# Two blocks of dense experts' activations put between the last scores and the one-hot rows, and weight loads put ahead of the last gate stores

## The chip, the cores and the metric

The kernel runs on one core of a Trainium2 chip. The metric is device time in microseconds of one execution. The profile is that of one execution, taken by the hardware profiler; times in it count from the start of its span. The engines are PE (matrix multiplication), DVE (vector), ACT (activation), POOL and SP; here SP only issues DMAs.

## The reference

For 2,048 tokens of 512 values the kernel computes `x + A(layernorm(x)) + B(layernorm(x))`. A is attention with 32 heads of 16 that share one key and one value head. B is a layer of 4,096 single-neuron experts: each token has, for each of 32 heads, two rows of 64 scores; the top two of each row give four candidate experts, the best two of these are kept, and

```python
g = _softmax(top_s, axis=-1)
ue = u[top_e]
ve = v[top_e]
act = _gelu(jnp.einsum("nd,nhkd->nhk", xf, ue))
out = jnp.einsum("nhk,nhk,nhkd->nd", g, act, ve)
```

All inputs and outputs are float32. Matmuls run on operands split into a high and a low half, three products (`TERMS`) for one.

## The kernel before

**Tiling.** The tokens are 16 tiles of 128, in four groups of four. Attention is a sequence of double steps (`att_steps`): 4 score matmuls (L318, `sc`), exponentials on ACT (L321, `pt`), 16 matmuls of probabilities with values (L332, `pv`) as the trace counts them, 4 more scores. In each step `mid()` puts out DVE's and ACT's work for the experts, and `fill()` lets a generator, `score_thread` (run by `run_scores`), put out PE's: so many matmuls for a step as the costs it yields (`yield cost`) leave room for, `yield None` ending the step's share. Instructions are written in this order by hand (`tc.manual_schedule`); no scheduler moves them. `STORES` is a list of DMAs that SP is to issue at the start of a following step. SP issues in order; in the built program its DMAs take turns on eight semaphores, so that an issue waits for the DMA eight before it.

**Experts, two ways.** The score thread computes for each group the scores in eight chunks (`item`, `psc` L532), of which DVE takes the top two (L545, L547, `batch`); `gates` (L635 to L643) forms the softmax. Groups 0 and 1 then gather the rows of u and v for each token and expert (POOL, L883), DVE multiplies and sums (`dots` L895, `adds` L930). These go on beside everything else: the dots' pace is the variable `pos`. Groups 2 and 3 are dense instead (`dense`): every token meets all 4,096 experts, in 32 blocks of 128, each weighted by a gate that is mostly zero. So the trace has two dense groups; the texts call them the first and the second.

**A dense group.** (1) After the last scores the indices and gates are transposed (`ptd`, L714) and copied into `tr` (L715). POOL first copies an index table `io` (L704). (2) For 32 stretches of 16 tokens DVE makes one-hot rows (`oa` L725; `ob` L727, times the gate L728) and PE multiplies them (`pg`, L752, 16 matmuls each): a gate for each token and expert. ACT copies these (`gst`, L757), and SP stores them to DRAM, eight pairs of 512 KB in runs of 256 bytes (L760); behind the last pair it loads the gates of the first blocks (`gy`, L675) and x (`da`, L739). (3) For each block: raw weights `rw` (L657, L658; two buffers, so raw 2 is loaded when raw 0 is split) are split by ACT (L687, high) and DVE (L688, low) into `wk`; 12 matmuls contract x with u (`pact`, L799); ACT and DVE form gelu and gate (Square L821, L822, times the gate L825, tanh L842, L828, halves of `wd` L831 and L835); and after each pair of blocks the sums with v (`pout`, L783, L786). Blocks 0 and 1 are split in the steps of the last two one-hot products (`later_split`). Attention's output goes through `pwo` (L427), added on DVE (L433) to partial sums that SP loads (`fin`, L420).

**Lists.** `BEHIND` is DVE's work that follows the next dots; `ON_ACT`, `LAST`, `LATER` and `LATER_ACT` hold ACT's work for this or the next step; `POST` the copies out of a product. `dense_on` tells `mid` which stage runs. The buffers in question: `wk` (8; also `io`, `tr` and the one-hot rows), `wqt` (2, raw weights), `gy` (3), `wd` (4, also `gst`), and three banks `x` of PSUM for `psc`, `ptd`, `pg`, `pact`, `pout` and `pwo`.

Of the kernel before, what the change touches and what calls it, by code (L numbers as in the profile page):

```python
# [23 lines left out]
P = 128  # L24
# [30 lines left out]
def tile_kernel(ctx, tc, x, wq, wkv, wo, wqT, kT, uv, ub, vb, out):  # L55
# [17 lines left out]
    d_w = [dram.tile([P, KC, 2, 512], F32, name=f"dw{c}") for c in range(NC)]  # L73
    d_g = dram.tile([NB, P, 512], F32, name="dg")
# [481 lines left out]
    DT = []  # L556
# [7 lines left out]
    def batch(ph, c, b):  # L564
# [52 lines left out]
        if c == 0:  # L617
            DT.clear()
            dense_tiles()
# [14 lines left out]
        def gates():  # L634
            V.tensor_scalar(den, ex, 2.0, 2.0, op0=OP.mult, op1=OP.add)  # L635
            gg = T("gd", F32, [P, BT, 8])
            gv = gg.rearrange("p t (h k) -> p t h k", k=2)
            V.reciprocal(gv[:, :, :, 0], den)
            V.tensor_mul(gv[:, :, :, 1], ex, gv[:, :, :, 0])
            gh = T("gh", F16, [P, BT, 8])  # L640
            V.tensor_scalar(gh, gg, GS, None, op0=OP.mult)
            V.tensor_copy(dgt[:, :, 0, w], gh)
            stt(dgt[:, :, 1, w], gg, GS, gh, op0=OP.mult, op1=OP.subtract)  # L643

# [3 lines left out]
    def dense(DG, after):  # L648

        df1, df2, dgt = DT[:3]  # L650
# [12 lines left out]
        def gate_tile(b):  # L663
            if b not in gates:
                gy = late[0].tile([P, 2, 512], F32, name="gy", tag="gy", bufs=3)
                gates[b] = gy
            return gates[b]

        def fetch_gates(b):
            if b < NB and b not in fetched:  # L670
                if formed[0] < b - 2:

                    store(lambda: fetch_gates(b))
                    return
                nc.sync.dma_start(gate_tile(b)[:, 0, :], d_g[b])  # L675
                fetched.add(b)

        splits, halved = {}, set()

        def split(b):  # L680
            if b < NB:
                if b not in raws:
                    run(STORES)
                rw = raws.pop(b)
                us, vs = wk_tile(), wk_tile()
                for i, w in enumerate((us, vs)):
                    nc.scalar.copy(w[:, 0, :], rw[:, i, :])  # L687
                    behind(lambda w=w, i=i: nc.vector.tensor_tensor(out=w[:, 1, :], in0=rw[:, i, :], in1=w[:, 0, :],  # L688
                                                                    op=OP.subtract))
                behind(lambda: halved.add(b))  # L690
                splits[b] = us, vs
# [11 lines left out]
        io = kt(F16, (P, P, TB))  # L703
        nc.gpsimd.tensor_copy(io, iota_h[:, :, None].to_broadcast([P, P, TB]))  # L704
        fetch(0)
        fetch(1)
        yield None
        tr = kt(F16, (P, 3, 512))
        for n, src in enumerate((df1, df2, dgt)):
            if n == 2:  # L710
                yield None
            p = xtile("ptd")
            for j in range(GT):
                nc.tensor.transpose(p[:, j * P:(j + 1) * P], src[:, j].rearrange("p r s -> p (r s)"), ident)  # L714
            nc.scalar.copy(tr[:, n, :], p)  # L715
            yield 0.45
        dense_on[0] = 2
# [3 lines left out]
        def onehot(q):  # L721
            if q < NQ:
# [3 lines left out]
                ob = kt(F16, (P, NB, TB))  # L726
# [4 lines left out]
        def first_gates():  # L731

            fetch_gates(0)
            fetch_gates(1)
# [6 lines left out]

        onehot(0)
        onehot(1)
        for q in range(NQ):
# [10 lines left out]
            def copies(pv_=pv_, st=st, ql=ql, t0=t0):  # L755
                for hb in range(2):
                    nc.scalar.copy(st[hb][:, :, ql * TB:(ql + 1) * TB], pv_[:, 16 * hb:16 * hb + 16, :])  # L757
                if ql == 3:
                    for hb in range(2):
                        store(lambda hb=hb: nc.sync.dma_start(  # L760
                            d_g[16 * hb:16 * hb + 16, :, t0:t0 + 64].rearrange("b p t -> p b t"), st[hb]))
# [11 lines left out]
        def sums():  # L773
# [4 lines left out]
            for j in range(GT):  # L778
                p = xtile("pout")
                n = 0  # L780
                for wd, vs in ready:
                    for a, c in TERMS:
                        nc.tensor.matmul(p, wd[:, a, j * P:(j + 1) * P], vs[:, c, :], start=n == 0, stop=n == 5)  # L783
# [7 lines left out]
        for b in range(NB):  # L791
            if b not in halved:
                flush()
            us, vs = splits.pop(b)
            p = xtile("pact")
            n = 0
            for k in range(KC):
                for a, c in TERMS:
                    nc.tensor.matmul(p, us[:, a, k * P:(k + 1) * P], XT[DG][k][:, c, :],  # L799
                                     start=n == 0, stop=n == 11)  # L800
                    n += 1
# [4 lines left out]
                if k == KC - 1 and b == NB - 1 and after is not None:  # L806
                    wp_read(after, range(2))
                if b == NB - 1 and after is not None:
                    load_phase2_xt(SEQ[after][0], k)
                if k < KC - 1:  # L810
# [12 lines left out]

            def gated(g=g, p=p):
# [4 lines left out]

            def high(y=y, wd=wd):  # L830
                nc.scalar.copy(wd[:, 0, :], y)  # L831
                behind(lambda: low(y, wd))
# [5 lines left out]
            def product(whole=whole, high=high, then=LATER_ACT.append):  # L838
                behind(whole)
                then(high)  # L840

            LAST.append(lambda y=y: nc.scalar.activation(y, y, AF.Tanh))  # L842
# [8 lines left out]
            held.append((wd, vs))  # L851
            yield 3 * UNIT
            if b == 0:
                yield None
            if b % 2:
                later_split(b + 2)
                if ready:
                    yield from sums()
                else:
                    yield None  # L860
                ready, held = held, []
# [139 lines left out]
    def score_thread():  # L1001
        for n, (ph, c) in enumerate(SEQ):
            if n < 2:
                yield from wp_make(c)
            make = wp_make(n + 1) if 0 < n < NC - 1 else iter(())
            for ti in range(TPH):
                yield from item(n, ti, make)
# [5 lines left out]
            if ph >= NSP and c == NC - 1:  # L1013
                yield from dense(ph, n + 1 if n + 1 < len(SEQ) else None)
# [132 lines left out]
    with tc.manual_schedule(engines={E_.PE, E_.Activation, E_.DVE, E_.Pool, E_.SP}):  # L1147
# [3 lines left out]
        for d in range(half + 24):  # L1151


            if d < half * 3 // 4:
                pos += 2.1 if len(IDX) < NC * TPH else (1.7, 2.5, 1.4)[dense_on[0]]
            else:
                pos += max(0.0, NSL - pos) / max(half - 4 - d, 1)
# [3 lines left out]
            def mid():  # L1161
# [20 lines left out]
                sums = min(a_ready[0] - a_next[0], max(todo, 3) if d < half else 4)  # L1182
                if dense_on[0] == 2:
# [78 lines left out]
```

## Time and profile before

| | |
|---|---|
| runs | 1992.95, 1997.14 and 2001.03 us; median 1997.14 |
| profiled execution | 2001.03 us, span 1999.3 us, mean granted clock 0.967 |
| busy | PE 1882.9 (94%), DVE 1682.7 (84%), ACT 1292.0 (65%), POOL 570.8 (29%) |
| DMA | 494.79 MB, mean 247 GB/s |
| chain that ended last | PE 63%, DVE 20%, DMA 5%, ACT 2%, issue 2% |

Busy times are sums over the span. In a row of a view, "waited for" is idle time of the engine directly before the instruction, with what released it; idle time of an engine that nobody waits for costs nothing. The granted clock is a share of full speed; at 0.5 a matmul takes twice as long. The first dense group lies between about 597 and 800 us of the span, with the end of its one-hot products at 741; the second between about 1439 and 1660, with that end at 1564.

### The profile page before, as it was taken

The page shows a single profiled execution, that of the slowest core. Times are in us where ns is not written, and L with a number is a line of the kernel's source. Part 1 is how long each engine was busy: PE and PEld are TensorE (multiplying, and loading weights), DVE is VectorE, ACT ScalarE, POOL GpSimd, SP SyncE. Part 2 cuts the span into 40 slices and gives each one's busy share as a digit, 9 for nine tenths or more (in the row PEclk, how much of TensorE's full clock was granted, in tenths as well). Part 3 has the DMA queues.
Part 4 walks back from the last instruction along what each step waited for, and adds up shares of the span by engine and source line. Part 5 has one row for each costly group of instructions (what it writes and reads, how often), then busy time and mean ns, then how long its engine had stood idle before and what let it go on. Part 6 is the DMA issues. An engine that isn't in the chain of part 4 may idle for free.

```text
span 1999.3 us, 34729 instructions
## 1 busy us (share of the span) xinstructions
PE 1882.9 (94%) x10990; PEld 997.5 (50%) x10990; DVE 1682.7 (84%) x6713; ACT 1292.0 (65%) x1804; POOL 570.8 (29%) x542
## 2 busy tenths in 40 slices
PE   6869999999998998999999999999899789999997
PEld 4534444555554444555555455555445345555552
DVE  7537888999998786999999779999999668999993
ACT  3236666655556785787877565555568567788873
POOL 2202232222222232333444222222223333333320
PEclk9989999999997998999999999999979899999999
DMA  7847878977664878888889877777568877888762
GB/s 272 301 185 235 276 272 272 331 275 248 218 212 140 229 221 271 264 269 269 284 297 328 286 253 261 268 238 225 176 169 234 276 245 263 268 277 257 263 211 63
DMA packets 239882, 494.79 MB, mean 247 GB/s; under 512 B 93380, under 2 KB 93380, under 8 KB 239692
## 3 DMA queue, kind: packets, MB, share of 16 engines
q0 software_dynamic: 73728, 268.47, 40.5%
q1 hardware_dynamic: 163960, 222.44, 34.0%
q10 hardware_dynamic: 2004, 1.61, 0.3%
q8 instruction: 88, 1.44, 0.3%
q14 instruction: 102, 0.84, 0.1%
HBM read 429.51 MB, written 57.64 MB: 244 GB/s over the span
## 4 chain that ended last, share of the span: by engine, by line
PE 63%; DVE 20%; DMA 5%; issue 2%; ACT 2%; SPq 1%; DVEq 0%; ACTq 0%
PE pv L332 18%; PE sc L318 12%; PE psc L532 10%; PE pout L783 8%; PE pact L799 8%; DVE i L547 5%; DVE xa L930 4%; DVE m L545 3%; DVE g L895 3%; PE pg L752 3%; PE pw L487 2%; PE pwo L427 1%; DMA dg<-gst 1%; ACT pt L321 1%; DMA fin<-dpart 1%
## 5 line engine op out<-in xcount | busy, mean ns | idle before, releaser
L321 ACT ACTIVATE pt<-sc 128x1024 f32<-128x1024 f32 x1024 | 993.0, 1025 | 471.1 <-PE sc L318 424.6
L883 POOL DMA_INDIRECT g<-in_uv_dram,idx x512 | 554.0, 1082 | 1358.4 <-DVE xa L930 697.4
L332 PE MATMUL pv<-pt,vaug 128*32 128x512 f32 x4096 | 524.1, 631 | 0.0
L318 PE MATMUL sc<-qa,kaug 64*128 64x512 f32 x2048 | 389.1, 454 | 14.4 <-ACT pt L321 13.5
L532 PE MATMUL psc<-wk,xt 128*128 128x512 f32 x1536 | 388.2, 400 | 5.3 <-DMA xt<-dxt 3.2
L930 DVE SCALAR_TENSOR_TENSOR xa<-g,w,xa 128x512 f32<-128x512 f32 x512 | 370.6, 745 | 0.0
L895 DVE CUSTOM_DVE_ANT_0 g<-g,xa 128x512 f32<-128x512 f32 x512 | 336.1, 681 | 3.0 <-DMA g<-in_uv_dram,idx 3.0
L532 PEld LDWEIGHTS psc<-wk,xt 128*128 128x128 f32 x1536 | 277.8, 188 | 108.7 <-issue 38.5
L318 PEld LDWEIGHTS sc<-qa,kaug 64*128 64x128 f32 x2048 | 157.6, 187 | 338.2 <-ACT pt L321 203.5
L332 PEld LDWEIGHTS pv<-pt,vaug 128*32 128x32 f32 x4096 | 110.7, 113 | 263.4 <-issue 261.7
L799 PE MATMUL pact<-xt,wk 128*128 128x512 f32 x768 | 198.7, 404 | 14.6 <-DVE fin L433 6.3
L547 DVE FIND_INDEX8 i<-m,psc 128x8 uint32<-128x64 f32 x1024 | 206.4, 221 | 0.0
L783 PE MATMUL pout<-wk,wd 128*128 128x512 f32 x768 | 195.7, 402 | 8.7 <-DVE wd L835 4.7
L799 PEld LDWEIGHTS pact<-xt,wk 128*128 128x128 f32 x768 | 141.1, 190 | 65.4 <-issue 17.7
L783 PEld LDWEIGHTS pout<-wk,wd 128*128 128x128 f32 x768 | 140.6, 188 | 56.7 <-DVE wd L835 6.0
L545 DVE MAX8 m<-psc 128x8 f32<-128x64 f32 x1024 | 146.0, 214 | 22.2 <-PE psc L532 19.8
L786 DVE TENSOR_TENSOR da<-da,pout 128x512 f32<-128x512 f32 x128 | 82.7, 679 | 8.2 <-PE pout L783 7.9
L918 DVE SCALAR_TENSOR_TENSOR w<-gth,ga 128x4 f32<-128x4 f32 x128 | 20.2, 158 | 79.9 <-ACT gth L911 79.4
L688 DVE TENSOR_TENSOR wk<-rw,wk 128x512 fp32r<-128x512 f32 x128 | 84.8, 682 | 0.1
L725 DVE TENSOR_TENSOR oh<-oh 128x2048 f16<-128x2048 f16 x64 | 78.0, 1219 | 7.1 <-PE pg L752 7.1
L752 PE MATMUL pg<-oh 128*128 128x32 f16 x1024 | 73.4, 246 | 8.1 <-DVE oh L728 8.1
L687 ACT CAST wk<-rw 128x512 fp32r<-128x512 f32 x128 | 73.6, 628 | 9.0 <-DMA rw<-in_ub_dram 6.7
(150 smaller groups left out, 1341.8 us busy)
## 6 DMA issues: line engine op xcount, KB each, us to landing
wk<-dw SPq DMA_DIRECT2D x96, 512.0 KB
wqt<-in_wqT_dram SPq DMA_DIRECT2D x32, 512.0 KB
dw<-wk SPq DMA_DIRECT2D x32, 512.0 KB
rw<-in_ub_dram SPq DMA_DIRECT2D x64, 256.0 KB
rw<-in_vb_dram SPq DMA_DIRECT2D x64, 256.0 KB
dg<-gst SPq DMA_DIRECT2D x32, 512.0 KB
gy<-dg SPq DMA_DIRECT2D x64, 256.0 KB
qa<-dqh SPq DMA_DIRECT2D x128, 64.0 KB
```

What stands on the lines that cost most here:

```text
L318: nc.tensor.matmul(p[:, b, :], kaug[o:o + 64, kc * P:(kc + 1) * P], QA[u][o:o + 64, i, :], start=True, stop=True)
L321: nc.scalar.activation(pt, p, AF.Exp, scale=SCALE)
L332: nc.tensor.matmul(PV[u][32 * j:32 * j + 32, :], vaug[:, kc, :], pt[:, b, :], start=kc == 0, stop=kc == 15)
L532: nc.tensor.matmul(p, XT[g][k][:, a, j * P:(j + 1) * P], WC[n_][k][:, bb, :], start=n == 0, stop=n == 11)
L545: nc.vector.max(m8[:, jb, s, :], p[:, s * E:(s + 1) * E])
L547: nc.vector.max_index(i8[:, jb, s, :], m8[:, jb, s, :], p[:, s * E:(s + 1) * E])
L752: nc.tensor.matmul(p[:, i * NB:(i + 1) * NB], oa[:, :, i], ob[:, :, i], start=True, stop=True)
L783: nc.tensor.matmul(p, wd[:, a, j * P:(j + 1) * P], vs[:, c, :], start=n == 0, stop=n == 5)
L799: nc.tensor.matmul(p, us[:, a, k * P:(k + 1) * P], XT[DG][k][:, c, :], start=n == 0, stop=n == 11)
L883: nc.gpsimd.indirect_dma_start(out=gt, out_offset=None, in_=uv, in_offset=bass.IndirectOffsetOnAxis(ap=IDX[ph, c, ti][:, s:s + 1], axis=0))
L895: nc.vector.tensor_tensor_reduce(u, u, XN[TPH * ph + ti], scale=1.0, scalar=0.0, op0=OP.mult, op1=OP.add, accum_out=a[:, i:i + 1])
L930: nc.vector.scalar_tensor_tensor(acc, v, w[:, i:i + 1], acc, op0=OP.mult, op1=OP.add)
```

## The change

- `io` is formed once, at the start, by an ACT copy, stored to DRAM (512 KB), and loaded into a `wk` buffer by SP in each dense group; POOL's copy is gone.
- `dense` is started as a generator at the last score chunk. At its first tile raw weights 0 and 1 are fetched, at the second the u halves of both are split (`early`), from the third on DVE does no dots and at most one add in a step (`dense_on` 3) until the one-hot rows begin.
- The contractions of blocks 0 and 1 (`first`) run between the last scores and the one-hot products, one before the transposes and one before or inside the first products; Square, a copy of the contraction and the gelu follow at once, kept in `hh`; the gate is multiplied in later (`scaled`).
- `ob` gets a tile of its own of three slots (one `wk` buffer).
- The remaining splits come at products 24 and 27 (v halves of blocks 0 and 1) and 31 (block 2), instead of 30 and 31 for blocks 0 and 1; so raw weights 2 and 3 are loaded before the last gate stores, and raw 4 behind them.
- The last gate store is cut into 3, 13 and 16 blocks; behind the 3 come the gates of blocks 0 to 2 and the x loads, then the rest.
- In the first blocks the sums come one block later, and blocks 3 and 4 are gated from `BEHIND`.

The diff, cut to its core:

```diff
...
+    d_io = dram.tile([P, P, 16], F16, name="dio")
...
+        io = gtile(F16, (P, P, 16))
+        nc.scalar.copy(io, iota_h[:, :, None].to_broadcast([P, P, 16]))
+        nc.sync.dma_start(d_io, io)
...
+        def gate_rows(b):
+            return gate_tile(b)[:, b if b < 2 else 0, :]
...
-                if formed[0] < b - 2:
+                if (b == 3 and multiplied[0] < 2) or (b > 3 and formed[0] < b - 2):
...
-                nc.sync.dma_start(gate_tile(b)[:, 0, :], d_g[b])
+                nc.sync.dma_start(gate_rows(b), d_g[b])
...
+        splits, halved, multiplied = {}, set(), [0]
+        def half_split(b, i):
+            rw, w = raws[b], wk_tile()
+            nc.scalar.copy(w[:, 0, :], rw[:, i, :])
+            behind(lambda: nc.vector.tensor_tensor(out=w[:, 1, :], in0=rw[:, i, :], in1=w[:, 0, :], op=OP.subtract))
+            return w
...
-                rw = raws.pop(b)
-                us, vs = wk_tile(), wk_tile()
-                for i, w in enumerate((us, vs)):
-                    nc.scalar.copy(w[:, 0, :], rw[:, i, :])
-                    behind(lambda w=w, i=i: nc.vector.tensor_tensor(out=w[:, 1, :], in0=rw[:, i, :], in1=w[:, 0, :],
-                                                                    op=OP.subtract))
+                us = half_split(b, 0) if b > 1 else None
+                splits[b] = us, half_split(b, 1)
...
-                splits[b] = us, vs
+                raws.pop(b)
...
-        io = kt(F16, (P, P, TB))
-        nc.gpsimd.tensor_copy(io, iota_h[:, :, None].to_broadcast([P, P, TB]))
...
-        yield None
-        tr = kt(F16, (P, 3, 512))
-        for n, src in enumerate((df1, df2, dgt)):
-            if n == 2:
-                yield None
+        yield 0.0
+        early = []
+        on_act(lambda: early.extend(half_split(b, 0) for b in range(2)))
+        yield 0.0
+        df1, df2, dgt = DT[:3]
+        def activations(b, us, p):
+            n = 0
+            for k in range(KC):
+                for a, c in TERMS:
+                    nc.tensor.matmul(p, us[:, a, k * P:(k + 1) * P], XT[DG][k][:, c, :],
+                                     start=n == 0, stop=n == 11)
+                    n += 1
+                yield k
+        def first(b):
+            p = xtile("pact")
+            for k in activations(b, early[b], p):
+                if k < KC - 1:
+                    yield 3 * UNIT
+            g, y = gate_rows(b), hh[:, b, :]
+            nc.scalar.activation(y, p, AF.Square, scale=C_CUB ** 0.5)
+            nc.scalar.copy(g, p)
+            nc.vector.scalar_tensor_tensor(y, y, C_IN, p, op0=OP.add, op1=OP.mult)
+            def go():
+                nc.scalar.activation(y, y, AF.Tanh)
+                behind(lambda: nc.vector.scalar_tensor_tensor(y, y, 1.0, g, op0=OP.add, op1=OP.mult))
+            LATER.append(go)
+            yield 3 * UNIT
+        def spread(n):
...
+        io = kt(F16, (P, P, TB))
+        nc.sync.dma_start(io, d_io)
+        tr = kt(F16, (P, 3, 512))
+        hh = late[0].tile([P, 2, 512], F32, name="gy", tag="gy", bufs=3)
+        yield from first(0)
+        for n in range(2):
+            spread(n)
...
+        while not gated_all:
+            yield None
+        spread(2)
+        yield 0.45
...
-                ob = kt(F16, (P, NB, TB))
+                ob = obs[:, q % 3]
...
-            fetch_gates(0)
-            fetch_gates(1)
+            for b in range(3):
+                fetch_gates(b)
...
+        obs = kt(F16, (P, 3, NB, TB))
...
+        yield from first(1)
...
-                    for hb in range(2):
-                        store(lambda hb=hb: nc.sync.dma_start(
-                            d_g[16 * hb:16 * hb + 16, :, t0:t0 + 64].rearrange("b p t -> p b t"), st[hb]))
-                    if t0 == 448:
-                        store(first_gates)
+                    cut = (0, 3, 16, NB) if t0 == 448 else (0, 16, NB)
+                    for b0, b1 in zip(cut, cut[1:]):
+                        store(lambda b0=b0, b1=b1: nc.sync.dma_start(
+                            d_g[b0:b1, :, t0:t0 + 64].rearrange("b p t -> p b t"),
+                            st[b0 // 16][:, b0 % 16:b0 % 16 + b1 - b0, :]))
+                        if b0 == 0 and t0 == 448:
+                            store(first_gates)
...
-                later_split(q - NQ + 2)
+            if q in (NQ - 8, NQ - 5, NQ - 1):
+                later_split((NQ - 8, NQ - 5, NQ - 1).index(q))
...
-            if b not in halved:
-                flush()
-            us, vs = splits.pop(b)
-            p = xtile("pact")
-            n = 0
...
-                if k == 0:
-                    store(lambda b=b: fetch_gates(b + 1) if b else None)
-                    if b % 2 == 0:
-                        later_split(b + 2)
...
-            wd = late[0].tile([P, 2, 512], F32R, name="wd", tag="wd", bufs=4)
-            if b > 1 and b not in fetched:
-                if formed[0] < b - 2:
...
+            if b > 1:
+                if b == 3:
+                    yield None
+                if b not in halved:
...
-                run(STORES)
-            gy = gate_tile(b) if b < 2 else gates[b]
+                p = xtile("pact")
+                for k in activations(b, splits[b][0], p):
+                    if k == 0:
+                        store(lambda b=b: fetch_gates(b + 1))
+                        if b % 2 == 0 and b != 4:
+                            later_split(b + 2)
...
+                if b not in fetched:
+                    if b > 3 and formed[0] < b - 2:
+                        flush()
+                    run(STORES)
+                    assert b in fetched
+            vs = splits.pop(b)[1]
+            gy = gates[b]
...
-            g, y = gy[:, 0, :], gy[:, 1, :]
-            nc.scalar.activation(y, p, AF.Square, scale=C_CUB ** 0.5)
-            stt(y, y, C_IN, p, op0=OP.add, op1=OP.mult)
+            g, y = (gy[:, 0, :], gy[:, 1, :]) if b > 1 else (gy[:, b, :], hh[:, b, :])
...
+            def scaled(y=y, g=g):
+                multiplied[0] += 1
+                stt(y, g, 1.0 / GS, y, op0=OP.mult, op1=OP.mult)
...
-                gated()
-                product()
-            elif b == 1:
-                behind(gated)
-                product()
+                nc.scalar.activation(y, p, AF.Square, scale=C_CUB ** 0.5)
+                stt(y, y, C_IN, p, op0=OP.add, op1=OP.mult)
+                LAST.append(lambda y=y: nc.scalar.activation(y, y, AF.Tanh))
+                if b in (3, 4):
...
+                    behind(lambda gated=gated, g=g, p=p: gated(g, p))
+                else:
+                    gated(g, p)
+                behind(whole)
+                LATER_ACT.append(high)
...
-                LATER.append(lambda gated=gated, product=product: (behind(gated), product(then=on_act)))
+                LAST.append(lambda scaled=scaled, high=high: (behind(scaled), on_act(high)))
...
-            yield 3 * UNIT
-            if b == 0:
-                yield None
+            if b > 1:
+                yield 3 * UNIT
...
-                if ready:
...
+                if b > 3:
...
-                else:
-                    yield None
-                ready, held = held, []
+                if b != 3:
+                    ready, held = held, []
+            elif b == 4:
+                yield from sums()
+                later_split(b + 2)
+                ready, held = held[:2], held[2:]
...
+            dn = None
+            if ph >= NSP and c == NC - 1:
+                dn = dense(ph, n + 1 if n + 1 < len(SEQ) else None)
+                yield next(dn)
...
+                if dn and ti == 1:
+                    yield next(dn)
+                if dn and ti == 2:
+                    dense_on[0] = 3
...
-                yield from dense(ph, n + 1 if n + 1 < len(SEQ) else None)
+                yield from dn
...
-                pos += 2.1 if len(IDX) < NC * TPH else (1.7, 2.5, 1.4)[dense_on[0]]
+                pos += 2.1 if len(IDX) < NC * TPH else (1.7, 2.5, 1.4, 0.0)[dense_on[0]]
...
-                pos += max(0.0, NSL - pos) / max(half - 4 - d, 1)
+                pos += max(0.0, NSL - pos) / max(half - 4 - d, 1) if dense_on[0] < 3 else 0.0
...
+                if dense_on[0] == 3:
+                    sums = min(sums, 1)
```

More of the change, by code (lines that the diff above doesn't have):

```diff
@@ L552, in tile_kernel @@
     IDX, G = {}, {}
-    DT = []
+    DT, gated_all = [], []
     def dense_tiles():
@@ L618, in batch @@
             DT.clear()
+            gated_all.clear()
             dense_tiles()
@@ L782, in sums @@
                     for a, c in TERMS:
-                        nc.tensor.matmul(p, wd[:, a, j * P:(j + 1) * P], vs[:, c, :], start=n == 0, stop=n == 5)
+                        nc.tensor.matmul(p, wd[0][:, a, j * P:(j + 1) * P], vs[:, c, :], start=n == 0, stop=n == 5)
                         n += 1
@@ L828, in whole @@
                 stt(y, y, 1.0, g, op0=OP.add, op1=OP.mult)
+            def scaled(y=y, g=g):
+                multiplied[0] += 1
+                stt(y, g, 1.0 / GS, y, op0=OP.mult, op1=OP.mult)
             def high(y=y, wd=wd):
-                nc.scalar.copy(wd[:, 0, :], y)
-                behind(lambda: low(y, wd))
+                wd.append(late[0].tile([P, 2, 512], F32R, name="wd", tag="wd", bufs=4))
+                nc.scalar.copy(wd[0][:, 0, :], y)
+                behind(lambda: low(y, wd[0]))
             def low(y, wd):
```

35 lines of the change are left out of this document (14 added, 21 removed).

## The prediction, made before the changed kernel was run

> **What bounds the kernel now.** I read the page first. PE is busy 94% of the span, so time is lost only where its row, or the granted clock below it, dips.
>
> ```profile
> span 1999.3 us, 34729 instructions
> ...
> PE   6869999999998998999999999999899789999997
> ...
> PEclk9989999999997998999999999999979899999999
> ```
>
> A slice is 50 us. Besides start-up, both rows dip around slices 13 to 16 and 29 to 33: the two dense groups. The view of busy time by windows shows it in 100-us stretches (columns: length, then PE, PEld, DVE, ACT, POOL, then granted clock, DMA share, GB/s).
>
> ```profile
> 600.00:700.00 100.00, 92.49 (x692) 43.42 (x690) 80.45 (x223) 68.92 (x110) 23.75 (x20) 0.86 0.65 184
> 700.00:800.00 100.00, 87.68 (x610) 44.15 (x610) 75.32 (x168) 73.70 (x114) 31.63 (x29) 0.91 0.79 245
> 800.00:900.00 100.00, 100.00 (x562) 56.62 (x554) 94.43 (x220) 80.07 (x117) 38.43 (x35) 1.00 0.81 267
> ...
> 1400.00:1500.00 100.00, 88.43 (x610) 46.15 (x606) 94.09 (x426) 61.13 (x91) 24.38 (x22) 0.87 0.56 171
> 1500.00:1600.00 100.00, 88.11 (x694) 43.85 (x690) 81.26 (x184) 70.74 (x115) 30.32 (x27) 0.89 0.89 257
> ```
>
> Outside these stretches PE is full at clock 1.00; inside, 5 to 12% is idle and 10% of the clock is missing. The waits, taken window by window, name the causes. At the start of a group (here the second) PE has no matmul to do while DVE finishes the last score batch:
>
> ```profile
> PE ptd L714 <- DVE da L631: 8.7, 1, 8.7
> ```
>
> At the end, PE has used up the last one-hot rows and the first blocks wait for loads queued behind the last gate stores (PE, then SP, first group):
>
> ```profile
> 765.77 3.01 PE L799 MATMUL pact<-xt,wk 128*128 128x512 f32 x12
> 773.77 1.22 PE L799 MATMUL pact<-xt,wk 128*128 128x512 f32 x2 [4.98 <-ACT wk L687]
> 778.24 2.07 PE L799 MATMUL pact<-xt,wk 128*128 128x512 f32 x4 [3.25 <-DVE wk L688]
> ```
> ```profile
> 745.58 10.97 SPq L760 DMA_DIRECT2D dg<-gst  x2
> 760.56 0.81 SPq L675 DMA_DIRECT2D gy<-dg  x2
> 761.42 1.85 SPq L739 DMA_DIRECT2D da<-in_x_dram  x4
> 763.31 0.43 SPq L657 DMA_DIRECT2D rw<-in_ub_dram  x1
> ```
>
> Raw weights 3 are issued 17.7 us after the gate stores; ACT casts them at 773.10. In the second group the load that ends last is another, of attention's partial sums (waits, then PE's order of time):
>
> ```profile
> DVE fin L433 <- DMA fin<-dpart: 25.3, 3, 12.9
> ```
> ```profile
> 1591.81 2.93 PE L799 MATMUL pact<-xt,wk 128*128 128x512 f32 x6 [6.34 <-DVE fin L433]
> ```
>
> DVE stands 12.87 us at L433, ACT 13.83 behind it, and PE 6.34.
>
> **The change part by part.** PE executes the same matmuls; only their order differs, in about 34 steps of the first dense group and 30 of the second.
>
> *First group, start.* The batch that PE waits for ends at 607.69. After, DVE has two more subtractions ahead of it (2 x 0.68 from L688) and fewer dots (0.67 each): I take it to end about 1 us later, 608.7. PE's wait stays near 5 us, but block 0's 12 contraction matmuls (3.0 us, the row at 765.77) come before it and block 1's 12 inside the following waits. The step that ended at 625.8 ends about 2.5 us later, with 6.0 us of contractions already done: **gain 3.5** (0 to 6).
>
> *First group, end.* The last one-hot product comes two steps later in order. From that step on, before needs until 756.5 for the same place, 3.0 of it contractions; so after gets there at about 756.5 + 2.5 - 3.0 = 756, and earlier by 1 to 3 since ACT, which made PE wait 2.5 us for exponentials there (L321), has two of the four casts (0.63 each) behind it: 754. Blocks 2 and 3 now have weights, so PE runs on for 14.5 us (two steps of attention at 3.4, 24 matmuls at 6.0, some ACT limit). Then it wants block 4, whose raw weights are queued behind everything: 3-row store, three gate loads, four x loads, 13- and 16-row stores. Before, the same bytes bar 256 KB took 773.1 - 745.58 = 27.5 us from the first store; of these some 5 went to raw weights and `rsb` issued just ahead, which after are landed by then. Adding 2.5 for the copies of the last gates (two exponentials of 1.03 and a pair of 0.66) gives 25. The low end is 20: alone, 1,897 packets of 256 B passed in 2 us (758 to 760). The high end is 35: beside gathers only 230 did (754 to 756). At 25 raw 4 lands at 779 and PE idles some 10 us; with the cast, the subtraction, their waits and six matmuls (4.5 us) it is at 783.5. Before has done 12 matmuls (3.0 us) fewer at 780.24, so the same work at 783.2, and waits 1.38 for `wd` afterwards: 784.6. The start's 3.5 is thus mostly given back: **1 gained in the whole group** (+7 at a landing of 20, with ACT's cover; -9 at 35).
>
> [...] The sum goes by the 27.5-us row.
>
> *Second group, start.* L704's POOL copy (1.90 us) is gone. Beside it DVE's L641 took 2.53 us instead of 0.18, in front of the last batch: 2.35 gained. Two dots less, two subtractions more cancel. The wait of 8.69 shrinks by 2.35 and by the 3.0 of block 0; block 1's 3.0 runs in the waits behind. Less the load on ACT of two copies (0.58 each): **gain 7** (3 to 9).
>
> *Second group, end.* After ends its one-hot products at about 1573.5 (before passes that place at 1577.6; 2 us gained in time, 3.0 of contractions moved, 1.2 of gate products added). From there to the end of the sixth `pout` triple, nine steps of 3.4 (4.1 where ACT's four exponentials bind) with three `pwo` of 3.7, 36 contractions at 9.0 and 42 sums at 10.4 make 65 us. Two of the `fin` loads now come before the last gate stores; the third still follows raw 4 on SP, so DVE stands at L433 again, some 13.5 to 27 us after the last product. As before, PE lasts 7.3 us beyond DVE: 6.5 idle, 1 more for smaller ones (before: 6.34, 1.77, 1.36 and 3.60), and 5 for a cold clock behind it (before: 13.65 us at 0.5 from 1599.71, costing 6.8). 1573.5 + 65 + 12.5 = 1651 against 1663.3: **12 in all** (4 to 20), 5 of them beyond the start.
>
> *Start-up.* One ACT copy of 128 x 2048 enters ahead of ACT's first work, where PE waits for `qsq` (longest wait 2.0). No row has it; an ACT row of 128 x 1024 takes 1.03, so about 2. Bounds 0 (it sits in a gap) and 3; I take **1.5 lost**. The 512-KB store and the two loads have 10 us of slack.
>
> *Held-back dots and adds.* During the start DVE does no dots and at most one add a step; some 7 of each return in the last dense stage, where DVE is at 92 to 94%. Fully paid: 7 x 1.35 = 9.5 us per group; hidden: 0. PE is at 100% there and one step has about 0.4 us of DVE left, over 20 steps or more, so nearer to hidden: **1.5 lost**. One-hot rows get three slots instead of five: DVE forms a pair in 2.07 us (1.22 + 0.42 + 0.43) and 32 products take some 124 us, 3.9 each, so I cost it at 0, or 2 if `pg`'s waits of 8.1 us grow by a quarter.
>
> Sum: 1 + 12 - 1.5 - 1.5 = 10 gained. The profiled run took 2001.03 (span 1999.3), 3.9 above the median of 1997.14; 1991.0 there is **1987.1** at the median, rounded to 1987.
>
> **Rivals.** (a) *The stall only moves.* Raw 4 lands 5 us later than taken, or the backlog is paid fully: group one loses 5, group two 5 of its 12. For it speaks that ACT's casts stand in order ahead of tanh and exponentials; against it, that DVE's stall stops the gathers. Time 1997.
> (b) *Slower: the in-order cast of raw 4.* If it lands over 35 us after the last product (the high bound, and past it with POOL gathering throughout), first-group PE idles 22 instead of 10, ACT holds up every exponential behind the cast, and in the second group, where the cast's place comes some 18 us after the last product, PE loses 10 more than taken. It decides from some 10 us late in both groups on; at 12 late, 12 and 10 (ACT then holds what `fin` held before) are lost on the forecast: 2009.
> (c) *Full cover.* Packets run as if alone (landing at 20) and `fin` 113 follows: of the 41 us idle in four stretches (7.5 in 600 to 620, 12.1 in 740 to 800, 10.5 in 1440 to 1460, 11.0 in 1560 to 1620; the forecast leaves about 30) only some 12 stay, and half of the cold time goes: 1965.
> (d) *Cold contractions.* The trace grants 0.5 in units of 3.41 us after waits (10.24 us from 1456.35, behind the 8.69). If the 24 contractions of each group start behind such waits and run at half rate, they cost 6 us more per group: 1998. [...] Against it: block 0's follow directly on the scores, when PE is warm.
>
> **How the numbers follow.** Forecast 0.58 (own range 1975 to 1997, a little over half of it, 0.31, under 1987.2), (a) 0.12, (b) 0.13, (c) 0.13, (d) 0.04. A measurement tells about 0.5%, 10 us, from no change. Faster: 0.31 + 0.13 = 0.44; slower: (b), 0.13; the same: 0.43. The range 1967 to 2004 leaves out (b) and half of (c), 0.195.
>
> **What would show it.** In after's profile: L704 gone and L641 at 0.18 throughout; PE's wait for L631 under 5 us in the second group and about 5 in the first; the first wait for weight casts at block 4 instead of block 3, about 10 us in the first group; one `fin` wait fewer in the second; first score of attention later by 0 to 3 us; `wd` and `pout` waits unchanged in the last stages. I am wrong upwards if raw 4 is cast over 30 us after the last product, and downwards if PE meets no wait over 4 us at either end.

## The result, and the profile after

The changed kernel takes 2013.88 us (median of 7 runs, 2006.63 to 2015.74), the kernel before 1998.67 (7 runs, 1992.95 to 2009.10): the ratio is 1.0068, with a 95% interval of 1.0046 to 1.0089. The forecast was 1987, faster by half a per cent; by the ratio, the change costs 13.6 us. The profiled execution of the changed kernel took 2006.63 us, the shortest of its seven, against 2001.03 before; so its own profile shows only 5.6 us of the loss, and a second pair of profiles was taken below.

The windows of the changed kernel, with the columns as before (length, PE, PEld, DVE, ACT, POOL, clock, DMA share, GB/s):

```profile
600.00:700.00 100.00, 94.90 (x745) 46.54 (x744) 78.18 (x228) 76.83 (x118) 19.68 (x15) 0.95 0.58 162
700.00:800.00 100.00, 78.58 (x578) 42.57 (x574) 71.11 (x158) 68.01 (x108) 29.57 (x25) 0.90 0.78 236
1100.00:1200.00 100.00, 95.68 (x497) 48.38 (x497) 67.50 (x360) 53.97 (x66) 25.63 (x26) 0.97 0.75 259
1400.00:1500.00 100.00, 93.39 (x664) 50.59 (x663) 90.25 (x432) 67.64 (x99) 17.95 (x17) 0.96 0.54 164
1500.00:1600.00 100.00, 94.73 (x707) 44.66 (x706) 89.31 (x208) 72.86 (x117) 36.65 (x31) 0.87 0.86 256
1600.00:1700.00 100.00, 79.70 (x419) 40.45 (x417) 69.70 (x160) 59.19 (x85) 34.19 (x30) 0.88 0.79 261
```

Two of these stretches in the kernel before:

```profile
1100.00:1200.00 100.00, 97.96 (x529) 49.11 (x528) 75.09 (x408) 58.85 (x71) 28.30 (x28) 1.00 0.78 269
...
1600.00:1700.00 100.00, 94.25 (x507) 47.95 (x503) 79.22 (x185) 69.61 (x99) 36.92 (x33) 0.97 0.76 253
```

The starts of both groups gained, as they were meant to: 600 to 700 rises from 92.49 to 94.90 busy at 0.95 of the clock instead of 0.86, and 1400 to 1500 from 88.43 to 93.39 at 0.96 instead of 0.87. The ends lost it: 700 to 800 falls from 87.68 to 78.58, and 1600 to 1700 from 94.25 to 79.70. PE's waits over the whole execution name what took over (total, times, longest; the last line is the first one's row in the kernel before):

```profile
PE sc L322 <- ACT pt L325: 25.9, 27, 14.8
PE pact L728 <- DVE wk L693: 15.7, 2, 14.3
...
PE ptd L753 <- DVE da L636: 6.6, 2, 3.9
```
```profile
PE sc L318 <- ACT pt L321: 13.5, 22, 1.8
```

The wait for the last score batch (`ptd`) is 2.65 us in the second group, where it was 8.69. In its place stand two of over 14 us that were not there. ACT's order of time at the first of them, and at the second:

```profile
758.91 1.12 ACT L692 CAST wk<-rw 128x512 fp32r<-128x512 f32 x2
770.80 1.21 ACT L692 CAST wk<-rw 128x512 fp32r<-128x512 f32 x2 [10.76 <-DMA rw<-in_ub_dram]
771.92 0.62 ACT L899 ACTIVATE gy<-gy 128x512 f32<-128x512 f32 x1
772.45 1.92 ACT L325 ACTIVATE pt<-sc 128x1024 f32<-128x1024 f32 x2
...
1603.54 1.14 ACT L692 CAST wk<-rw 128x512 fp32r<-128x512 f32 x2
1617.72 1.25 ACT L692 CAST wk<-rw 128x512 fp32r<-128x512 f32 x2 [13.05 <-DMA rw<-in_ub_dram]
```

Both times ACT has cast raw weights 3 and stands at the cast of raw weights 4, which have not landed; tanh and attention's exponentials are behind it in its order. In the first group PE then stops in block 3, whose weights ACT had cast at 758.91 (PE, then DVE):

```profile
759.58 0.73 PE L728 MATMUL pact<-xt,wk 128*128 128x512 f32 x2 [0.66 <-ACT wk L692]
774.59 5.82 PE L728 MATMUL pact<-xt,wk 128*128 128x512 f32 x16 [14.28 <-DVE wk L693]
```
```profile
772.58 0.69 DVE L881 SCALAR_TENSOR_TENSOR gy<-gy 128x512 f32<-128x512 f32 x1 [8.92 <-ACT gy L899]
773.18 0.75 DVE L991 SCALAR_TENSOR_TENSOR xa<-g,w,xa 128x512 f32<-128x512 f32 x1
773.85 0.69 DVE L693 TENSOR_TENSOR wk<-rw,wk 128x512 fp32r<-128x512 f32 x1
```

PE has done two of the twelve matmuls of block 3 and lacks the low half of its weights. DVE forms that half (L693) behind a product (L881) that needs the tanh, and ACT has the tanh behind the cast of raw 4. So PE waits for raw 4 by way of ACT's order and DVE's, without needing it yet; the sixteen matmuls that follow are the other ten of block 3 and six of block 4. In the second group PE needs no weights at that moment, only exponentials, and stands all the same:

```profile
1604.19 0.96 PE L728 MATMUL pact<-xt,wk 128*128 128x512 f32 x3
1619.95 1.71 PE L322 MATMUL sc<-qa,kaug 64*128 64x512 f32 x4 [14.80 <-ACT pt L325]
```

Why raw 4 is that late, SP's order shows (second group; the last one-hot product ended at 1577.2):

```profile
1580.91 0.34 SPq L438 DMA_DIRECT2D out_dram<-fin  x1
1583.53 0.33 SPq L424 DMA_DIRECT2D fin<-dpart  x1
1583.94 0.26 SPq L309 DMA_DIRECT2D qa<-dm  x1
...
1590.29 0.30 SPq L314 DMA_DIRECT2D qa<-dql  x1
1590.69 0.38 SPq L814 DMA_DIRECT2D dg<-gst  x1
1597.56 1.29 SPq L685 DMA_DIRECT2D gy<-dg  x3
1598.89 2.35 SPq L790 DMA_DIRECT2D da<-in_x_dram  x4
1601.28 7.84 SPq L814 DMA_DIRECT2D dg<-gst  x2
1609.22 3.60 SPq L663 DMA_DIRECT2D rw<-in_ub_dram  x1
```

The first, small part of the last store is issued 13.5 us after the product. ACT's copy of the last gates ends at 1580.48; from there the store stands behind an output, a `fin` load and eight loads of `qa` for attention. Then 6.9 us pass until it has landed and the gates can be loaded; 3.7 for gates and x; 7.9 to issue the other two parts; 8.5 to issue and land raw 4. That is 40.5 us. In the first group the same five steps take 0.9, 5.6, 3.4, 7.0 and 6.5 us: 23.4.

**Where the time lies.** Attention's exponentials (1,024 in all, 128 x 1024 each) are the same in every kernel, so the time from the n-th to the m-th (counted from 0) is a stretch of equal attention work. For two profiles of each kernel, in us:

| stretch (number of the exponential) | before | before, again | changed | changed, again |
|---|---|---|---|---|
| first group and what follows, 240 to 500 | 464.2 | 458.6 | 461.3 | 465.9 |
| weights for the next scores, 535 to 600 | 116.1 | 114.5 | 122.1 | 121.7 |
| 600 to 700 | 175.5 | 175.5 | 173.7 | 173.7 |
| second group, 700 to 900 | 370.1 | 373.6 | 372.3 | 375.5 |

By the means, the first group loses 2 us, the second 2, and 6.6 go in a place where the prediction had nothing, near 1113 us, after the first group has ended; 600 to 700 gives back 1.8. With 2 ahead of the 240th exponential these make 11 of the 11.2 us between the mean spans (2004.9 and 2014.8 against 1999.3 and 1998.1). PE's wait there, and what SP waited for ahead of these loads (between 1085 and 1122 us; SP stands until an output store has landed):

```profile
PE psc L536 <- DMA wk<-dw: 3.1, 2, 2.4
```
```profile
SPq L424 <- DMA out_dram<-fin: 10.2, 1, 10.2
```

Besides these 3.1 us of idle time, the clock was granted at 0.5 for 6.83 us from 1116.6 on, and 15 score matmuls took 6.32 us where 15 take 3.70 at full speed.

### The profile page after: what moved, and what is told of

It reads as the page before. It is cut to its first block, busy times and chain, and to the rows that moved or that the text cites. A ratio compares the mean times of both kernels' runs of the same rounds, so it can differ in the third digit from the quotient of the medians.

```text
span 2004.9 us, 34733 instructions
## 1 busy us (share of the span) xinstructions
PE 1876.4 (94%) x10990; PEld 998.8 (50%) x10990; DVE 1679.9 (84%) x6713; ACT 1295.8 (65%) x1809; POOL 574.7 (29%) x540
## 4 chain that ended last, share of the span: by engine, by line
PE 43%; DVE 11%; DMA 3%; ACT 2%; issue 1%; SPq 0%; DVEq 0%; ACTq 0%
PE pv L336 12%; PE pout L839 8%; PE sc L322 8%; PE pact L728 8%; PE psc L536 4%; DVE i L551 2%; DVE xa L991 2%; DVE g L956 2%; DVE m L549 2%; PE pwo L431 1%; ACT pt L325 1%; PE pg L805 1%; DMA out_dram<-fin 1%; DMA dg<-gst 0%; DMA fin<-dpart 0%
## 5 line engine op out<-in xcount | busy, mean ns | idle before, releaser
L944 POOL DMA_INDIRECT g<-in_uv_dram,idx x512 | 561.7, 1097 | 1364.7 <-DVE xa L991 664.2
L336 PE MATMUL pv<-pt,vaug 128*32 128x512 f32 x4096 | 513.7, 620 | 0.0
L692 ACT CAST wk<-rw 128x512 fp32r<-128x512 f32 x128 | 73.9, 628 | 24.0 <-DMA rw<-in_ub_dram 23.8
L693 DVE TENSOR_TENSOR wk<-rw,wk 128x512 fp32r<-128x512 f32 x128 | 85.4, 687 | 0.0
L979 DVE SCALAR_TENSOR_TENSOR w<-gth,ga 128x4 f32<-128x4 f32 x128 | 20.6, 161 | 74.3 <-ACT gth L972 73.7
L551 DVE MATCH_VALUE_LOAD i<-m,psc 128x8 f32 x1024 | 81.1, 79 | 0.0
```

The source lines that it names most:

```text
L336: nc.tensor.matmul(PV[u][32 * j:32 * j + 32, :], vaug[:, kc, :], pt[:, b, :], start=kc == 0, stop=kc == 15)
L551: nc.vector.max_index(i8[:, jb, s, :], m8[:, jb, s, :], p[:, s * E:(s + 1) * E])
L693: behind(lambda: nc.vector.tensor_tensor(out=w[:, 1, :], in0=rw[:, i, :], in1=w[:, 0, :], op=OP.subtract))
L944: nc.gpsimd.indirect_dma_start(out=gt, out_offset=None, in_=uv, in_offset=bass.IndirectOffsetOnAxis(ap=IDX[ph, c, ti][:, s:s + 1], axis=0))
```

## The experiments

Theory A: the loss is raw weights 4, late behind the last gate stores, with ACT in order behind them. Theory B: it is the dots and adds held back. Theory C: the DMA engines are full at the end of a group, and any order of the loads only moves the wait. Ratios are to the kernel before, with 95% intervals.

**e1, raw 4 between x and the rest of the stores.**

```diff
-                        store(lambda b0=b0, b1=b1: nc.sync.dma_start(
+                        put = REST.append if b0 and t0 == 448 else store
+                        put(lambda b0=b0, b1=b1: nc.sync.dma_start(
...
                 store(lambda: fetch(b + 2))
+                if b == 2:
+                    STORES.extend(REST)
```

> The changed kernel, but raw weights 4 are issued behind the x loads and ahead of the 13- and 16-block parts of the last gate store, instead of behind them. Theory A (the loss is the in-order wait of ACT for raw 4 behind these stores: 10.8 and 13.1 us at the cast, 14.3 and 14.8 us on PE): the two waits of ACT fall to 4 us or less, and the time falls by 10 to 20 us against the changed kernel, to 0.995 to 1.002 of the kernel before. Theory B (the loss is from dots and adds held back): both casts earlier, but less than 4 us in the time. Theory C (the DMA engines are simply full there): the waits only move, to gates of block 3 or to the partial sums, and the time stays within 4 us.

1.0052 (1.0020 to 1.0084). ACT's waits at casts fall from 23.8 to 14.1 us, the longest to 7.4, PE's longest from 14.3 and 14.8 to 9.9 and 9.1. Two fifths of the casts' wait went with the 13- and 16-block stores; raw 4 was still behind the round trip of the first part and the x loads. By the centres the time is 3 us below the changed kernel: less than the 10 to 20 of A, and within the 4 us that C allowed, so e1 does not decide between them.

**e2, dots and adds not held back.**

```diff
-                if dn and ti == 2:
-                    dense_on[0] = 3
```

> The changed kernel without the stretch in which DVE does no dots and at most one add a step. Theory A: the start of a group loses some of its gain (1 to 3 us each), the waits for raw 4 stay at 10 us or more, the time stays within 4 us of the changed kernel. Theory B: the 3.1 us that PE waits for score weights near 1113 us, and the half-rate clock behind it, are gone, and the time falls by 6 to 12 us.

1.0101 (1.0045 to 1.0156). The wait near 1113 us is gone, as B said (stretch 535 to 600: 116.3), but the time does not fall, so B fails: the stretch 240 to 500 grows to 473.5. By the centres the hold pays more at the start of a group than it costs later, though the intervals overlap (four runs here).

**e3, the last store not cut in three.**

```diff
-                    cut = (0, 3, 16, NB) if t0 == 448 else (0, 16, NB)
+                    cut = (0, 16, NB)
...
-                        if b0 == 0 and t0 == 448:
+                        if b0 and t0 == 448:
                             store(first_gates)
```

> The changed kernel with the last gate store in two parts of 16 blocks, as before, and the first gate and x loads behind both. Theory A: raw 4 still comes after the same bytes, so the casts wait as long (9 to 14 us), and the gates of block 2 come later besides; the time is 0 to 6 us above the changed kernel. Theory C: fewer small transfers, so 0 to 5 us below it.

1.0039 (1.0010 to 1.0068): 6 us below the changed kernel by the centres, at the edge of what can be told. The longest cast wait is 9.2 us instead of 13.0. The three parts do not help. This is the way that C expected (0 to 5 us below), and not A's (0 to 6 above).

**e4, the index table alone, on the kernel before.**

```diff
-        nc.gpsimd.tensor_copy(io, iota_h[:, :, None].to_broadcast([P, P, TB]))
+        nc.sync.dma_start(io, d_io)
```

> The kernel before with one part of the change alone: the index table is formed once at the start by ACT, stored, and loaded by DMA in each dense group, in place of POOL's copy. All theories: DVE's instruction beside the copy falls from 2.53 to 0.18 us in the second group, which gives 2 us there; the start of attention comes 1.8 us later; together 0 within 2 us.

1.0004 (0.9976 to 1.0033). No row of `gh` is over 0.183 us any more, where one was 2.53; the gain and the cost at the start are both inside the spread.

**e5, raw 4 ahead of every part of the last store.** The third split comes two products sooner, so its buffer is free sooner:

```diff
-            if q in (NQ - 8, NQ - 5, NQ - 1):
-                later_split((NQ - 8, NQ - 5, NQ - 1).index(q))
+            if q in (NQ - 8, NQ - 5, NQ - 3):
+                later_split((NQ - 8, NQ - 5, NQ - 3).index(q))
```

> The changed kernel with the splits at products 24, 27 and 29 instead of 24, 27 and 31, so that raw weights 4 are issued ahead of every part of the last gate store in both groups. Theory A (waiting for raw 4 behind the last stores is the loss): ACT's waits at the cast of raw 4 (10.8 and 13.1 us, 7.4 with raw 4 between x and the rest of the stores) fall under 3 us, PE's 14.3 and 14.8 us to under 6, the time falls by 10 to 20 us against the changed kernel. Theory C (the bytes of the last stores, the first gates and x have to pass before PE can go on, in whatever order): PE waits as long in sum, now for gates or partial sums, and the time falls by under 6 us.

1.0001 (0.9975 to 1.0027): 13 us below the changed kernel, all of its loss. PE's longest wait for exponentials is 1.5 us instead of 14.8, and the longest cast wait 3.4:

```profile
PE sc L322 <- ACT pt L325: 14.6, 27, 1.5
```

Theory A had the cast waits under 3 us. What is left in the second group is the load that the prediction had named: DVE waits for `fin`, and PE 7.25 us behind it.

```profile
DVE fin L437 <- DMA fin<-dpart: 16.1, 3, 12.1
```
```profile
1624.09 5.84 PE L728 MATMUL pact<-xt,wk 128*128 128x512 f32 x12 [7.25 <-DVE fin L437]
```

For the second group A stands and C falls: the same bytes in another order cost less, and the stretch 700 to 900 is 366.6 us against 372.3 and 375.5. In the first group the waits rather moved, as C had it: PE still waits 4.65 us in block 3 and then 7.00 for `wd` (2.82 in the changed kernel), and the stretch 240 to 500 is 462.8 against 461.3 and 465.9. So the profile, taken of the slowest of ten runs, places 7 of the 13 us; where the others are is open. The edit also moves the split of block 2 two products ahead; no run has that without the new place of raw 4.

**e6, the held-back dots made good during the one-hot products; e8, that and raw 4 ahead.**

```diff
-                pos += 2.1 if len(IDX) < NC * TPH else (1.7, 2.5, 1.4, 0.0)[dense_on[0]]
+                pos += 2.1 if len(IDX) < NC * TPH else (1.7, 2.5, 1.75, 0.0)[dense_on[0]]
```

> The changed kernel, but DVE's dots run at 1.75 a step instead of 1.4 during the one-hot products, so that the 8 dots held back at a group's start are made good there. Theory B: PE's wait of 3.1 us for score weights near 1113 us and the half-rate clock behind it (6.2 us together) are gone; against that DVE delays some one-hot rows by 1 to 3 us; the time falls by 3 to 6 us. Theory A: no change within 3 us, the stall near 1113 us may stay or go.

> Both edits together: raw weights 4 ahead of the last stores, and the held-back dots made good during the one-hot products. Theories A and B together: 1.000 to 0.990 of the kernel before. Theory C: 1.003 or more.

1.0134 (1.0102 to 1.0165) and 1.0061 (1.0040 to 1.0083): each 12 to 13 us above the same kernel without the edit, against all that A and B expected. C's 1.003 or more for e8 came out, but the loss is the same in e6, where raw 4 is behind the stores: it belongs to this edit. The count of dots is back to that of before (252 at exponential 500 in both), yet the wait near 1113 us is not gone but longer, 6.2 and 7.3 us, now with SP waiting 11.8 us for `dinv` ahead of the loads. So it is not the number of dots that makes this wait. That DVE's time during the one-hot products is not free is the likely reading of the 12 us; the profiles do not place them.

**e7, the hold alone, on the kernel before** (from the last tile's scores on, added where `dense_on` is set in the changed kernel).

```diff
+                if ph >= NSP and c == NC - 1 and ti == 3:
+                    dense_on[0] = 3
                 yield from item(n, ti, make)
```

> The kernel before with one part of the change alone: no dots and at most one add a step, here from the last tile's scores until the one-hot rows. Theory B: a start of each group 2 to 4 us sooner, and in exchange a wait for score weights near 1113 us with a cold clock behind it, 4 to 6 us; the time 0 to 4 us above the kernel before. Theory A: the start's gain alone, 2 to 6 us below the kernel before.

0.9997 (0.9975 to 1.0018). The wait near 1113 us appears in the kernel before too: 6.7 us (535 to 600: 125.1), SP 9.5 us behind an output store. The second group gains (364.4), so the sum is nothing.

**e9, raw 4 ahead and the hold from the fourth tile on; e10, raw 4 ahead and the store not cut.**

> The changed kernel with raw weights 4 ahead of the last gate stores, and with DVE's dots and adds held back from the fourth tile's scores of the last chunk on instead of the third. If the wait for score weights near 1113 us comes from the hold by where it puts the outputs of finished tiles in SP's order, a shorter hold moves them and the wait of 3 us and its cold clock go (6 us); the start loses 1 to 3 us a group; together 0.995 to 1.000 of the kernel before. If the wait comes from something else in the change, it stays, and the time is 1.001 to 1.004.

> The changed kernel with raw weights 4 ahead of the last gate stores, and these in two parts of 16 blocks, the first gate and x loads behind both. If the cut brings the first gates sooner and PE waits for gates once raw 4 is there, 3 to 8 us above the same kernel with the cut. If PE waits for partial sums and exponentials whatever the cut, within 3 us of it.

e9: 1.0064 (1.0039 to 1.0088), the wait near 1113 us at its longest, 8.7 us; a shorter hold does not remove it, and the time is above both ranges given. e10: 1.0006 (0.9985 to 1.0027), the same as e5; the cut changes nothing.

**e11 and e12, both kernels once more** for the table above.

> The changed kernel once more, for a second profile. Theory A: ACT's waits at the cast of raw 4 again over 7 us in each group, PE's longest wait for exponentials or weight halves again over 9 us. If these waits vary by 5 us or more between two executions, that is where the spread of the times lies.

> The kernel before once more, for a second profile. All theories: PE's wait for the last score batch near 9 us in one of the groups, no wait for score weights near 1113 us, and the time within 6 us of its first profile.

2016.50 and 1999.77 us. The waits for raw 4 are there again: ACT 20.6 us in two casts, the longest 11.7; PE 13.4 and 12.5. The kernel before has no wait of PE over 5 us for weights in a dense group in either of its two profiles.

**e13, raw 4 ahead, the hold in the second group alone; e14, raw 4 ahead, no hold.**

```diff
-                if dn and ti == 2:
+                if dn and ti == 2 and ph > NSP:
```

> The changed kernel with raw weights 4 ahead of the last gate stores, and with DVE's dots and adds held back in the second dense group alone. If the wait for score weights near 1113 us is an effect of the hold in the first group, it goes (6 us less there), the first group's start loses 2 to 6 us, and the second group is as in the kernel with raw 4 ahead and both holds: 0.996 to 1.002 of the kernel before. If the wait comes from another part of the change, it stays and the time is 1.001 to 1.005.

> The changed kernel with raw weights 4 ahead of the last gate stores and no dots or adds held back at all. If the hold alone makes the wait near 1113 us, it is gone here too; the starts of both groups lose 2 to 6 us each against the kernel with both holds, so 1.000 to 1.005 of the kernel before. If the wait is there, the hold is not its cause.

1.0044 (1.0020 to 1.0068) and 1.0041 (1.0017 to 1.0065). The stretch 535 to 600 is 117.6 and 118.0; over all profiles it is 114.5 to 118.7 in the six without a hold in the first group and 121.5 to 126.2 in the ten with one. So the hold of the first group makes the wait near 1113 us. e13's time is above the range given for that (0.996 to 1.002); its first group lost as much: without the hold 240 to 500 takes 468.2 and 470.0 instead of 462.8 (e5), and over the profiles of changed kernels 468.2 to 473.5 in the three without it against 455.3 to 465.9 in the seven with it (e6 and e8 aside). So by these stretches the hold is worth having; the times say so by their centres alone (e14 against e5), as the intervals overlap.

## Why the prediction was wrong

Between the forecast and the mean spans lie some 21 us: 14 in the second group, 3 in the first, 5 from the hold, less the 1.8 that came back from 600 to 700.

**Raw 4 in the second group: the step that failed.** The prediction took 25 us from the last product to the landing of raw 4, worked out on the first group, gave the second group no landing of its own, and counted the second group's end as `fin` alone: PE "lasts 7.3 us beyond DVE: 6.5 idle". The landing took 40.5 us, the cast of raw 4 stood ahead of the exponentials, and PE idled 14.80. Most of the 15 us more lie in SP's order: the last store is queued behind attention's `qa` loads in the second group (13.5 us) and not in the first (0.9). In the kernel before, these loads came 34 us behind the store (1602.97 against 1568.58). The change ends the one-hot products later in attention's order, behind 808 exponentials instead of 800; the prediction saw this for two `fin` loads, but not for the `qa` loads that follow the second of them. The group came out 2 us longer instead of 12 shorter. With raw 4 ahead (e5) the step holds as written: 7.25 idle behind `fin`, and the group takes 366.6 us against 371.9, the mean of before. So 7 us of the miss are raw 4 there. Some 7 more are the rest of that end: in e5 PE's smaller waits between the last product and the sixth triple of `pout` are 6.7 us, where 1 was taken.

Rival (b), at a chance of 0.13, named this in-order cast and gave 2009. Its condition came about in the second group alone, with 7 us instead of its 10; its 12 us in the first group did not come. That its time is near the measured one is in part luck: the 6.6 us near 1113 and the smaller waits of the second end, which it did not have, stand in for these 12.

**Raw 4 in the first group: about the size, by another way.** The landing was taken at 25 us and was 23.4. PE idled 14.28 us, where some 10 were forecast and about 3 more for cast and subtraction. But "Blocks 2 and 3 now have weights, so PE runs on" failed: the first wait did not move on to block 4. PE stopped two matmuls into block 3, 12.9 us after the last product and not 14.5, because DVE had the low half of block 3 behind a product that waited for ACT. The gain of 1 us forecast for the group was a loss of 2, within the scatter of two profiles.

**The hold: mis-sized, by its place.** It was priced at 1.5 us, as DVE work that returns in the last dense stage. It did not return there: at the 700th exponential DVE was still 7 dots behind (338 instead of 345). Instead 6.6 us went where nothing had been looked at. That the hold of the first group causes it is shown (e2, e7, e13, e14). How is not shown: it seems to shift what SP waits for to just ahead of the weights for the next scores, but this was an output store in most kernels and `dinv` in e6 and e8, SP waits 6.6 us for `dinv` there in the kernel before as well, and giving the dots back did not remove the wait.

**Starts: right.** The wait for the last batch fell from 8.69 to 2.65 us in the second group (under 5 forecast). In the first it is 3.92 (about 5 forecast), but it did not "stay" there: the row at 607.69 in the kernel before has 0.72, and it grew while the idle time of 600 to 620 fell from 7.51 to 4.74 us. With POOL's copy gone, no row of `gh` is over 0.182 us, where one was 2.53 in the kernel before. The contractions did not run cold: in the first group the clock was at 0.5 for one unit of 3.41 us, behind the first transposes, and block 0's and block 1's twelve matmuls took 3.02 and 3.01 us, so rival (d) did not come.

**The start of the execution.** 1.5 us were forecast for the added copy. The first exponential comes about 1 us later by the means of the two pairs, but over all kernels with the table it lies anywhere from 147.2 to 152.4 us, so no run tells this term.

Two things in the prediction were misread. The instants given for cold stretches (1456.35, 1599.71) are counted from another zero than the span and lie 10.6 us late; the durations are right. And the 13.65 us at 0.5 did not cost 6.8: at 1589.1 to 1602.7 they lie in part within the wait of 6.34 us, and PE was busy for 9.05 us of them, which makes some 4.5, an estimate from half of the busy time (the sixteen `pv` matmuls at 1598.14, within the stretch, took 3.64 us, where they take 1.92 at full clock).

## What to carry to other kernels

A load that is needed next must be ahead of the stores in its queue, not behind them: here 13 us hung on the place of two DMAs, and of the split that frees their buffer, in the order of issue, and cutting the store in front of them did not help. The waits of ACT's casts for raw 4, 10.76 and 13.05 us, held what stood behind them in ACT's order, so such a wait is priced by what stands behind it (here attention's exponentials, and a tanh that DVE waited for; PE idled 14.28 and 14.80 us) and not by who needs its result. When the same step occurs twice, work out the order of each queue for each occurrence as it will be in the changed program: the second had eight small loads in front that neither the first nor the kernel before had there.

## What the runs showed of the hardware

The issue of a store kept SP: the last 16-block part of the second group, 2,048 runs of 256 bytes, held it for 7.08 us with gate and x loads in front of it, where the median of all 34 issues of these stores is 0.59. So raw 4 was late by SP's own time too. And PE's two long waits cost more than their length. The clock was granted at 0.5 for 17.07 us from 761.59 on, 1.3 us into the 14.28 us in the first group; 4.1 of them fell after PE had gone on, and sixteen matmuls took 5.82 us instead of 4.0, an estimate from the twelve of this form that take 3.02 at 603.19. In the second group it was at 0.5 for 17.07 us from 1608.09 on, of which 5.2 fell after the 14.80 us; there sixteen `pv` matmuls, at 1621.59, took 3.64 us, where they take 1.92 at full clock.
